# One subtraction of the first q, on its fourth slot, is moved from VectorE to POOL

## The chip, the cores and the metric

The kernel runs on one core of a Trainium2 chip, with a granted TensorE clock of 0.999. The metric is device time in microseconds (us), lower is better. Engines are called by the names that the profile uses: PE (TensorE matmul), PEld (its weight load), DVE (VectorE), ACT (ScalarE), POOL (GpSimd), SP (SyncE).

## What is computed

An attention of the "efficient" kind, whose output is the input of a two-layer feed-forward net with an ELU between the layers. Everything is float32 at the outside.

```python
# q, k, v: [8 batches, 8 heads, 576 rows, 64]
q_s = softmax(q, axis=-1)          # over the 64 columns of each row: max, subtract, exp, sum, divide
k_s = softmax(k, axis=2)           # over the 576 rows
kv  = einsum('bhsd,bhse->bhde', k_s, v)
attn = einsum('bhsd,bhde->bhse', q_s, kv)
x   = attn.transpose(0, 2, 1, 3).reshape(4608, 512)
h   = x @ w_in                     # w_in: 512 x 2048
g   = where(h > 0, h, exp(min(h, 0)) - 1)
out = g @ w_out                    # w_out: 2048 x 512
```

## The kernel before

Each batch gives 512 rows to the net in one pass of 16 hidden tiles (128 hidden units by 512 rows); the 64 rows left over of each batch are gathered into a ninth pass. For one hidden tile PE runs four matmuls with `W1S` (`hidden_mm`, L911), ACT the exponential into `ES` (L894, or L891 and L892 for the tiles of a list), POOL a small fix-up of `ES` (L895), DVE the combination of both into `GT` (`elu`, L924), and PE four matmuls with `W2S` that add to the output (`project`, L932). Projection runs three tiles behind. The softmaxes and small attention matmuls of the next batch are woven between these tiles by the tables `FIRST`, `SECOND` and `LATER`, written by hand: words such as `qsub:2:dve` name a step, a part and an engine.

The first batch has nothing to hide behind. Its steps are the words of one string, `START`, and `first_batch` issues them in that order. An engine executes its own instructions in the order of issue, and waits by semaphores for what it reads and overwrites (`op`, `need`). So the string fixes four or five queues at once: a word that moves in it moves in the queue of its own engine only, among the words of that engine.

In the first batch q and k lie in four slots of two heads each. For slot n of q the steps are `qmax:n` (DVE, L671), `qsub:n` (subtract the row's maximum in place in `QR`, L678), `qexp:n` (ACT, L683), `qsum:n` (sum and reciprocal, DVE, L688 and L690), `qmul` (times the reciprocal, into `QS`, as float16, L707: `qmul:A:dve` for slots 0 and 1 together on DVE, `qmul:2:gp` and `qmul:3:gp` on POOL). `pturn:A` and `pturn:B` turn `QS` on PE (L765), `pwide:A` and `pwide:B` copy that into `QT` on ACT (L787). On the side of k and v, `kexp` makes the exponentials (ACT, L537 and L532), `vconv:A` and `vconv:B` convert v into `VB` (ACT, L854, and POOL, L856), `kv:A` and `kv:B` multiply them (PE, L559), and `kfac:A` (DVE) and `kfac:B` (its reciprocal on DVE, L613, the scaling on ACT, L622) write `MB`. `att:f` multiplies `MB` with `QT` (PE, L804), `xc:f` copies the result into `XT` (L811 on DVE, L813 on ACT), and `h:2:4` and `h:0:2` start the first hidden tiles. `warm` is a matmul whose result is not used. `kmax2:AB` and the `qmax` behind it on DVE belong to the second batch.

The words `w1:a:b` and `w2:a:b` load chunks of the two weight matrices; they are DMAs issued by POOL (L255, L262), and each takes time in POOL's own queue. The loads of q, k and v are issued by SP (L277, L285, L293).

Before the change `qsub:0` and `qsub:2` run on POOL (word `gp`) and `qsub:1` and `qsub:3` on DVE. In DVE's queue `qsub:3` stands between `qsum:0` and `qmul:A`. In POOL's queue the order from there on is `qsub:2`, `w2:2:3`, `w1:6:9`, `vconv:B`, `qmul:2`, `qmul:3`, `w2:3:4`, `w2:4:6`. The later batches subtract k's maximum in `ksub`; all words for its part `R` that reach the lines below `b == 1` name `dve`.

Of the kernel before, what the change touches and what calls it, by code (L numbers as in the profile page):

```python
# [11 lines left out]
B, H, S, D = 8, 8, 576, 64  # L12
# [3 lines left out]
R = 4  # L16
# [29 lines left out]
         "w1:4:6 kacross:B kexp:S vconv:A:act kmin:A qsub:2:gp diag:act:B w2:2:3 qsum:0 kmin:B "  # L46
         "kexp:A load:V:0:3 kmin:T qexp:2 qsub:3:dve qmul:A:dve qsum:2 load:V:0:2 qexp:3 w1:6:9 "
         "qsum:3 vconv:B:gp load:K:1:M qmul:2:gp kexp:B kexp:T kv:A kfac:A:dve pturn:A kv:B "
         "pwide:A:act kfac:B:act warm:1:3 att:1 att:0 qmul:3:gp pturn:B xc:1:dve xc:0 h:2:4 "
         "pwide:B:act w2:3:4 att:2 att:3 xc:2 load:Q:1:A load:Q:1:R w2:4:6 h:0:2 xc:3 kmax2:AB ")  # L50
# [70 lines left out]
class Gen:  # L121
# [303 lines left out]
    def ksub(self, b, part, en="gp"):  # L425
        if b == 1:
            self.ksub_slot(part, en)
            return
        e, s = self.E[en], b % 2
        KR = self.KR[s]  # L430
        nm = self.NB[:, :].rearrange("p (h d) -> p h d", d=64)
        if part != "R":
            h0, n = {"A": (0, 4), "B": (4, 4)}.get(part) or (2 * int(part), 2)
            kv = KR[:, 4 * h0:4 * (h0 + n), :].rearrange("p (h r) d -> p h r d", r=R)
            m = nm[:, h0:h0 + n, :].unsqueeze(2).broadcast_to([128, n, R, 64])
            keys = self.kkeys(b, part)
            self.op(en, lambda: e.tensor_tensor(kv, kv, m, ALU.subtract), keys + ["NB"], keys)  # L437
        else:
            for i in range(2):
                sl = slice(64 * i, 64 * i + 64)  # L440
                kv = KR[sl, 32:36, :]
                m = nm[sl, 4 * i:4 * i + 4, :]
                self.op(en, lambda: e.tensor_tensor(kv, kv, m, ALU.subtract),
                        [f"KR{s}R{i}", "NB"], [f"KR{s}R{i}"])
# [762 lines left out]
```

## Time and profile before

| | us |
|---|---|
| three runs: median (lowest to highest) | 310.6 (310.38 to 311.41) |
| the profiled execution, device time | 310.93 |
| its span, first to last instruction | 308.9 |
| PE busy in the span | 297.4 (96%) |
| DVE busy | 237.0 (77%) |
| ACT busy | 193.2 (63%) |
| POOL busy | 170.4 (55%) |

The profiled execution has 2.03 us outside its span, and is 0.33 us above the median of the three runs. Line numbers are those of the kernel before; after the change, lines from 429 on are one higher. A row of the timeline gives the start in us, the duration in us, the engine, the line, the operation, its output and inputs with their shapes, how many instructions are merged in it, and in brackets how long the engine sat idle before and who released it. Rows of one engine overlap by up to 0.1 us, since the next instruction is taken up before the one in front of it has ended. The chain of waits is followed back from the last instruction; its rows are stretches that do not overlap.

### The profile page before, as it was taken

The page shows a single profiled execution, that of the slowest core. Times are in us where ns is not written, and L with a number is a line of the kernel's source. Part 1 is how long each engine was busy: PE and PEld are TensorE (multiplying, and loading weights), DVE is VectorE, ACT ScalarE, POOL GpSimd, SP SyncE. Part 2 cuts the span into 40 slices and gives each one's busy share as a digit, 9 for nine tenths or more (in the row PEclk, how much of TensorE's full clock was granted, in tenths as well). Part 3 has the DMA queues.
Part 4 walks back from the last instruction along what each step waited for, and adds up shares of the span by engine and source line. Part 5 has one row for each costly group of instructions (what it writes and reads, how often), then busy time and mean ns, then how long its engine had stood idle before and what let it go on. Part 6 is the DMA issues. An engine that isn't in the chain of part 4 may idle for free.

```text
span 308.9 us, 4839 instructions
## 1 busy us (share of the span) xinstructions
PE 297.4 (96%) x1733; PEld 239.8 (78%) x1733; DVE 237.0 (77%) x401; ACT 193.2 (63%) x358; POOL 170.4 (55%) x214
## 2 busy tenths in 40 slices
PE   6769999999999999999999999999999999999995
PEld 4457877688878888888888888888888888888884
DVE  6999998979959898899889998998895353335442
ACT  2578785577468885877587758775777543334432
POOL 2856785596535742786378636863696333333440
PEclk9999999999999999999999999999999999999999
DMA  7999999995707994668565856590503030003004
GB/s 229 397 346 334 373 360 272 255 250 166 205 3 227 271 233 129 210 133 209 157 208 147 207 148 198 146 187 23 172 17 62 2 136 0 0 2 136 0 0 136
DMA packets 60583, 51.63 MB, mean 167 GB/s; under 512 B 26896, under 2 KB 50704, under 8 KB 60560
## 3 DMA queue, kind: packets, MB, share of 16 engines
q1 hardware_dynamic: 52960, 41.23, 47.8%
q0 software_dynamic: 6400, 8.39, 10.3%
q10 hardware_dynamic: 1200, 1.72, 2.2%
q8 instruction: 13, 0.21, 0.3%
q14 instruction: 10, 0.08, 0.1%
HBM read 38.27 MB, written 9.45 MB: 154 GB/s over the span
## 4 chain that ended last, share of the span: by engine, by line
PE 90%; DVE 6%; DMA 2%; issue 1%; SPq 1%; ACT 0%
PE bank L932 43%; PE bank L911 42%; PE bank L826 2%; DMA QR<-in_q_dram 2%; DVE KT L326 2%; PE bank L597 1%; DVE QF L688 1%; DVE QS L707 1%; DVE QF L671 1%; PE bank L804 1%; SPq L277 1%; PE bank L559 0%; DVE QR L678 0%; DVE QM L671 0%; DVE KA L326 0%
## 5 line engine op out<-in xcount | busy, mean ns | idle before, releaser
L932 PE MATMUL bank<-W2S,GT 128*128 128x512 f32 x572 | 153.5, 392 | 0.2 <-DVE GT L924 0.2
L895 POOL TENSOR_SCALAR ES<-ES 128x512 f32<-128x512 f32 (+1 forms) x130 | 85.6, 661 | 116.2 <-ACT ES L894 116.1
L911 PE MATMUL bank<-XT,W1S 128*128 128x512 f32 x512 | 138.4, 393 | 0.8 <-issue 0.6
L924 DVE SCALAR_TENSOR_TENSOR GT<-bank,ES 128x512 fp32r<-128x512 f32 (+1 forms) x130 | 88.0, 681 | 53.1 <-PE bank L911 38.4
L932 PEld LDWEIGHTS bank<-W2S,GT 128*128 128x128 f32 x572 | 106.2, 188 | 22.3 <-DVE GT L924 0.6
L894 ACT ACTIVATE ES<-bank 128x512 f32<-128x512 f32 (+1 forms) x130 | 76.1, 593 | 70.3 <-PE bank L911 70.2
L911 PEld LDWEIGHTS bank<-XT,W1S 128*128 128x128 f32 x512 | 94.1, 188 | 20.2 <-ACT XT L813 0.9
L678 POOL TENSOR_TENSOR QR<-QR,QM 128x512 f32<-128x512 f32 (+1 forms) x21 | 24.9, 1188 | 0.6 <-DVE QM L671 0.6
L683 ACT ACTIVATE QR<-QR 128x1024 f32<-128x1024 f32 (+3 forms) x19 | 19.1, 1007 | 3.3 <-DVE QR L678 3.1
L854 ACT ACTIVATE XT<-bank 128x320 fp32r<-128x320 f32 (+1 forms) x30 | 15.0, 500 | 9.4 <-PE bank L826 9.4
L688 DVE TENSOR_REDUCE QZ<-QR 128x16 f32<-128x1024 f32 (+1 forms) x14 | 18.8, 1343 | 0.6 <-ACT QR L683 0.6
L671 DVE TENSOR_REDUCE QM<-QR 128x16 f32<-128x1024 f32 (+1 forms) x14 | 18.8, 1341 | 0.0
L911 PE MATMUL bank<-XTR,W1S 128*128 128x512 f32 x64 | 16.6, 389 | 0.0
L622 ACT ACTIVATE MB<-bank,KZ 64x64 fp32r<-64x64 f32 x44 | 10.1, 303 | 7.4 <-DVE KZ L613 7.3
L437 DVE TENSOR_TENSOR KR<-KR,NB 128x512 f32<-128x512 f32 x16 | 14.6, 938 | 0.0
L387 DVE TRANSPOSE_TENSOR_REDUCE KM<-KR 128x32 f32<-128x1024 f32 x12 | 14.4, 1225 | 0.0
L856 POOL CAST QT<-QW 128x1024 fp32r<-128x1024 f16 x12 | 12.5, 1038 | 2.7 <-DMA QW<-QS 2.7
L911 PEld LDWEIGHTS bank<-XTR,W1S 128*128 128x128 f32 x64 | 12.0, 188 | 2.5
L891 ACT ACTIVATE ES<-bank 128x512 f32<-128x512 f32 x15 | 8.9, 594 | 6.7 <-PE bank L911 6.7
L826 PE MATMUL bank<-QT,MB 128*128 128x320 f32 (+1 forms) x48 | 12.4, 300 | 0.7 <-ACT XT L854 0.7
L707 POOL TENSOR_TENSOR QS<-QR,QI 128x1024 f16<-128x1024 f32 (+1 forms) x7 | 12.5, 1786 | 0.4 <-DVE QI L690 0.4
L483 ACT ACTIVATE EK<-KR 128x1024 bf16<-128x1024 f32 x12 | 12.6, 1051 | 0.0
(108 smaller groups left out, 263.6 us busy)
## 6 DMA issues: line engine op xcount, KB each, us to landing
out_dram<-OSB SPq DMA_DIRECT2D x30, 256.0 KB, 2.7
KR<-in_k_dram SPq DMA_DIRECT2D x6, 1024.0 KB, 8.3
VR<-in_v_dram SPq DMA_DIRECT2D x6, 1024.0 KB, 6.2
QR<-in_q_dram SPq DMA_DIRECT2D x5, 1024.0 KB, 8.1
KR<-in_k_dram SPq DMA_DIRECT2D x8, 288.0 KB, 6.4
VR<-in_v_dram SPq DMA_DIRECT2D x8, 288.0 KB, 6.8
W1S<-in_moe_w_in_dram POOLq DMA_DIRECT2D x3, 768.0 KB, 9.5
QR<-in_q_dram SPq DMA_DIRECT2D x4, 512.0 KB, 9.7
```

The lines of the kernel that those rows point to most:

```text
L671: self.op("dve", lambda: v.tensor_reduce(m, QR, AX.X, ALU.max), self.qkeys(b, part), self.qstat("QM", b, part))
L678: self.op(en, lambda: e.tensor_tensor(QR, QR, m, ALU.subtract), keys + self.qstat("QM", b, part), self.qown(b, part))
L683: self.op("act", lambda: a.activation(QR, QR, AF.Exp), keys, self.qown(b, part))
L688: self.op("dve", lambda: v.tensor_reduce(z, QR, AX.X, ALU.add), self.qkeys(b, part), self.qstat("QZ", b, part))
L707: self.op(en, lambda: e.tensor_tensor(out, QR, z, ALU.mult), keys + self.qstat("QI", b, part), [f"QS{x}" for x in cells])
L826: last = pe.matmul(self.bank[bank][:, a - c0:b - c0], self.MB[f][:, :, :].rearrange("p u d -> p (u d)"), self.QT[:, f, a - f * S:b - f * S ...
L854: self.op("act", lambda: e.activation(out, src, AF.Copy), reads, writes)
L894: self.op("act", lambda: a.activation(ES[:, x], ps[:, x], AF.Exp), [f"bank{bank}"], keys + mark)
L895: self.op("gp", lambda: g.tensor_scalar(ES[:, x], ES[:, x], -1.0, 1.0, ALU.add, ALU.mult), keys, keys)
L911: return pe.matmul(ps, self.W1S[:, kc, c * 128:(c + 1) * 128], x[:, kc, 0:SM], start=(kc == 0), stop=(kc == 3))
L924: self.op("dve", lambda: v.scalar_tensor_tensor(out[:, x], *how), [f"bank{bank}"] + eks + (["FINE"] if n < FINE else []), keys)
L932: return pe.matmul(self.bank[OB[t]][:, :], self.GT[n % NG][:, t * 128:(t + 1) * 128], self.W2S[:, c, :], start=(c == 0), stop=(c == NCH - ...
```

## The change

The word `qsub:3:dve` is taken out of its place in front of `qmul:A:dve`, and `qsub:3:gp` is put directly behind `qsub:2:gp`, in front of the loads `w2:2:3` and `w1:6:9` in POOL's queue. A second edit sets the engine of `ksub` to DVE where the part is `R`; every such word names DVE already.

```diff
-         "w1:4:6 kacross:B kexp:S vconv:A:act kmin:A qsub:2:gp diag:act:B w2:2:3 qsum:0 kmin:B "
-         "kexp:A load:V:0:3 kmin:T qexp:2 qsub:3:dve qmul:A:dve qsum:2 load:V:0:2 qexp:3 w1:6:9 "
+         "w1:4:6 kacross:B kexp:S vconv:A:act kmin:A qsub:2:gp qsub:3:gp diag:act:B w2:2:3 qsum:0 kmin:B "
+         "kexp:A load:V:0:3 kmin:T qexp:2 qmul:A:dve qsum:2 load:V:0:2 qexp:3 w1:6:9 "
          "qsum:3 vconv:B:gp load:K:1:M qmul:2:gp kexp:B kexp:T kv:A kfac:A:dve pturn:A kv:B "
          "pwide:A:act kfac:B:act warm:1:3 att:1 att:0 qmul:3:gp pturn:B xc:1:dve xc:0 h:2:4 "
@@ ksub
         if b == 1:
             self.ksub_slot(part, en)
             return
+        en = "dve" if part == "R" else en
         e, s = self.E[en], b % 2
```

## The prediction

> **What bounds the kernel now.** I read the page's busy times first, then PE's waits from 26.7 us to the end, then the chain of waits over the first 40 us.
>
> ```profile
> PE 297.4 (96%) x1733; PEld 239.8 (78%) x1733; DVE 237.0 (77%) x401; ACT 193.2 (63%) x358; POOL 170.4 (55%) x214
> ...
> PE bank L826 <- ACT XT L854: 0.7, 1, 0.7
> PE bank L911 <- ACT XT L813: 0.2, 1, 0.2
> PE bank L932 <- DVE GT L924: 0.2, 1, 0.2
> ...
> 14.47 1.31 DVE QR L678
> 15.78 2.08 DVE QS L707
> ...
> 26.27 0.44 DVE GT L924
> 26.75 1.20 PE bank L932 x4
> ```
>
> The first row would say "PE, leave the rest alone". The three rows of waits sharpen it: after 26.7 us PE waits 1.1 us in all. So from the first projection at 26.75 us on, PE's work is packed, and whatever brings that moment forward or back moves the end with it, unless a later wait eats it. The last four rows say what sets that moment: before it the chain is on DVE, and the subtraction that the change moves (L678 at 14.47, `qsub:3`) is a link of it, directly in front of `qmul:A` (L707).
>
> **DVE: what is removed.** These are DVE's rows behind it.
>
> ```profile
> 14.39 1.39 DVE L678 TENSOR_TENSOR QR<-QR,QF 128x512 f32<-128x512 f32 x1
> 15.70 2.16 DVE L707 TENSOR_TENSOR QS<-QR,QF 128x1024 f16<-128x1024 f32 x1
> 17.78 0.67 DVE L688 TENSOR_REDUCE QF<-QR 128x8 f32<-128x512 f32 x1
> ...
> 18.61 0.64 DVE L688 TENSOR_REDUCE QF<-QR 128x8 f32<-128x512 f32 x1
> ...
> 19.55 0.61 DVE L628 SCALAR_TENSOR_TENSOR MB<-bank,KZ 64x128 fp32r<-64x128 f32 x2
> ```
>
> One instruction goes, and 1.31 us of the chain with it. But two durations here look long, so I looked for the same shapes elsewhere, and for what happens when DVE and POOL both work.
>
> ```profile
> 27.05 0.68 DVE L678 TENSOR_TENSOR QR<-QR,QM 128x512 f32<-128x512 f32 x1
> 75.95 1.21 DVE L707 TENSOR_TENSOR QS<-QR,QI 128x1024 f16<-128x1024 f32 x1
> ...
> 132.94 1.10 DVE L437 TENSOR_TENSOR KR<-KR,NB 128x512 f32<-128x512 f32 x1
> ...
> 132.18 1.31 POOL L437 TENSOR_TENSOR KR<-KR,NB 128x512 f32<-128x512 f32 x1
> 133.44 1.07 POOL L895 TENSOR_SCALAR ES<-ES 128x512 f32<-128x512 f32 x1
> ```
>
> Undisturbed, a DVE subtraction of this shape is 0.68 and a product of `qmul:A`'s size 1.21 us. The last three rows show the disturbance: the DVE subtraction from 132.94 ends at 134.04, 0.6 behind the end of POOL's own subtraction at 133.49. It stood still until POOL's instruction was over and then ran its usual length; and POOL's next instruction (1.07) stood behind DVE in turn. So a DVE operation with two inputs in SBUF and a POOL operation take turns, whole instructions at a time, and a waiting DVE instruction goes ahead of POOL's next one. By these rows `qsub:3` lost 0.71 us and `qmul:A` 0.95 us to POOL.
>
> **POOL: what is added.**
>
> ```profile
> 13.09 1.06 POOL L678 TENSOR_TENSOR QR<-QR,QF 128x512 f32<-128x512 f32 x1
> 14.09 0.58 POOL L262 DMA_DIRECT2D W2S<-in_moe_w_out_dram  x1
> 14.66 0.75 POOL L255 DMA_DIRECT2D W1S<-in_moe_w_in_dram  x1
> 15.40 1.38 POOL L856 CAST VB<-VR 128x1152 bf16<-128x1152 f32 x1
> 18.78 2.04 POOL L707 TENSOR_TENSOR QS<-QR,QF 128x512 f16<-128x512 f32 x2 [2.00 <-DVE QF L690]
> ```
>
> The same instruction on POOL is 1.06 us (`qsub:2`, the first row). Its input is ready: DVE was past the maxima when it took up the old `qsub:3` at 14.39. So it runs from 14.15 to 15.2, and everything behind it in POOL's queue moves by 1.06: the issue of `w2:2:3` and `w1:6:9`, then `vconv:B`, which starts at 16.46. `qmul:2` and `qmul:3` have cover, since POOL sat idle between 16.78 and 18.78.
>
> **The new order of the start.** `qmul:A` is taken up at 14.47, and now POOL's `qsub:3` is in its way until 15.2. Then it goes ahead of `vconv:B` by the rule of turns and needs 1.21: it ends at 16.4, where it ended at 17.86, so 1.46 earlier. From the end of `qmul:A` to the end of `kfac:A` (20.16 in the rows above) lie 2.30 us of DVE work, so `kfac:A` ends at 18.7. Whether its inputs come in time is read from ACT and PE.
>
> ```profile
> 15.23 1.21 ACT L683 ACTIVATE QR<-QR 128x512 f32<-128x512 f32 x2
> 17.30 0.28 ACT L532 ACTIVATE EK<-bank 128x128 bf16<-128x128 f32 x1
> 18.64 1.02 ACT L787 ACTIVATE QT<-bank 128x1024 fp32r<-128x1024 f16 x1 [1.07 <-PE bank L765]
> 20.39 1.04 ACT L622 ACTIVATE MB<-bank,KZ 64x64 fp32r<-64x64 f32 x4 [0.72 <-DVE KZ L613]
> 21.46 0.60 ACT L813 ACTIVATE XT<-bank 128x512 fp32r<-128x512 f32 x1
> ...
> 18.44 0.73 PE L559 MATMUL bank<-VB,EK 64*64 64x66 bf16 x36
> 19.10 0.50 PE L1092 MATMUL bank<-GT,ONES 128*128 128x512 f32 x1
> 20.21 0.74 PE L804 MATMUL bank<-QT,MB 128*128 128x512 f32 x2 [0.60 <-DVE MB L628]
> ```
>
> ACT's `qexp:2` and `qexp:3` end at 16.44 as before: `qexp:3` can start no earlier than behind `qexp:2`, so the earlier `qsub:3` (15.2 for 15.78) brings nothing there; `qsum:2` needs only `qexp:2`, done about 15.84, and `qsum:3` about 17.2 finds its input. ACT is busy until 17.58 (second row). `pwide:A` started 0.78 behind the end of `qmul:A`; that would be 17.2, so ACT's queue holds it until 17.58, and it ends at 18.6 instead of 19.66.
>
> `att:1` (PE, 20.21) needs `kfac:A` (18.7), `pwide:A` (18.6), and stands in PE's queue behind `kv:B` and `warm`. That is the link that becomes the last. `kv:B` needs `vconv:B`. Undisturbed I take `vconv:B` at 1.17, scaled from POOL's converting copy of a slightly smaller tile:
>
> ```profile
> 64.86 1.04 POOL L577 CAST VB<-VR 128x1024 bf16<-128x1024 f32 x1
> ```
>
> 1.04 x 1152 / 1024 = 1.17, and its own row, 1.38, which has a turn of DVE in it, is the other end. So it ends between 17.63 and 17.84, and `kv:B` starts about then instead of 18.44 (ACT's last exponential, 17.58, is in time). From the start of `kv:B` to the end of `warm` were 1.16 us (18.44 to 19.60): PE is free for `att:1` between 18.85 and 19.05. Hence `att:1` comes 1.15 to 1.35 earlier; 1.25 is the middle.
>
> The rest follows it. `xc:1` and the second batch's maxima on DVE stand back to back up to the first `elu` at 26.27. On ACT `kfac:B` starts behind its reciprocal, about 18.95, ends about 20.0, and `xc:0` ends about 20.6 instead of 22.06: earlier by more than 1.25, so no brake. `qmul:2` and `qmul:3` start at 17.84 and end at 19.9 instead of 20.82, and `pturn:B` and `pwide:B` fit behind `xc:0`. The first projection comes 1.25 earlier.
>
> **What could take it back later.** The weights come in one queue in order of issue. The tightest use that I found is the load of chunks 9 to 12 of `W2S`.
>
> ```profile
> W2S<-in_moe_w_out_dram POOLq DMA_DIRECT2D x1, 1024.0 KB, 14.4
> ...
> 30.31 0.75 POOL L262 DMA_DIRECT2D W2S<-in_moe_w_out_dram  x1
> ...
> 45.63 1.18 PE L932 MATMUL bank<-W2S,GT 128*128 128x512 f32 x4
> ```
>
> Issued at 30.31, it lands at 44.7, and PE wants it at 45.63: 0.9 us to spare. It is issued behind POOL's work on the first tiles, so its issue moves with them; if the landing moves too, nothing is lost, and if it stays, PE waits 1.25 - 0.9 = 0.35. I take 0.05. For the two loads that POOL now issues 1.06 later I see no cost: loads issued there take 10 us and more to land behind older ones (14.4 us for the big one). The second edit is nothing, since no instruction changes its engine.
>
> The sum: 1.25 - 0.05 = 1.2 us earlier. The profiled execution would be 310.93 - 1.2 = 309.73; it stands 0.33 above the median of the runs, so the median becomes 309.4. Bounds of the unknown terms alone: a gain of 0.8 (`vconv:B` at 1.38, the weights' 0.35) to 1.4, thus 309.2 to 309.8. About 0.3%, 0.93 us, is what a measurement of this kernel can tell from no change, so this is just over it.
>
> **The rivals.**
>
> First, an unseen hold in front of `qmul:A`. The row of `qsub:3` speaks for it: it stood 0.7 us from 14.47 to 15.16, when POOL's rows show only the issue of two DMAs (14.15 to 15.40). Something of POOL kept the way closed; perhaps parts of POOL were already at `vconv:B`. The Trainium skill, "GPSIMD Engine Reference", section "4. When to use GPSIMD", says that a pair of POOL's cores makes the descriptors of a DMA; the others could then have gone on, which no run here shows. If such a hold also follows the new `qsub:3`, `qmul:A` ends 0.7 later, at 17.1, `kfac:A` at 19.4, and `att:1` at 19.45 instead of 20.21: a gain of 0.76, median 309.85. Against it stand the rows from 132.18, where the waiting DVE went first. The Trainium skill, "SBUF — State Buffer", section "Who interferes with whom", says that the order of issue decides who is blocked, and for the whole instruction; by that rule `qmul:A` goes first and the sum stays, and those rows agree. Chance 0.2.
>
> Second, the other side: the turn is lost altogether. If `qmul:A` still stands at 16.46, when `vconv:B` is taken up, it stands until 17.84 and ends at 19.05, 1.19 later than before; `kfac:A`, `att:1` and all behind them follow: 310.6 + 1.2 = 311.8. The point from which it decides is plain: `qmul:A` must get its turn by 16.65 (17.86 - 1.21), or the change costs time. For it: `qmul:A` did wait out most of `vconv:B` before the change (2.16 for 1.21). Against it: that time `vconv:B` was first at 15.40. Chance 0.13.
>
> Third, the gain arrives at 26.75 and the weights take it back: the landing at 44.7 stays, and further loads behind it stay too. With one such wait of 0.35 and a second of as much, 0.5 us is left: 310.1. For it: the 0.9 us to spare is less than the gain. Against it: those loads are issued by the same tiles that come earlier. Chance 0.13.
>
> **How the numbers follow.** The forecast has what remains, 0.54; its time is 309.4. Faster by over 0.3% is most of the forecast (0.45, as a gain of 0.8 to 0.93 and the spread of the runs take some of it) and a part of the first rival (0.08): 0.53. Slower by over 0.3% is the second rival and a little for the spread: 0.15. Within 0.3%: 0.32. The range reaches from 308.9, a gain of 1.46 as on `qmul:A` itself with a little for the spread, to 311.0, which takes in the first and third rival and the case of no gain; the second rival lies outside.
>
> **What would show it.** Right, if in the profile after POOL has two rows of L678 behind each other from 13.1 to 15.2, `qmul:A` on DVE ends near 16.4 and lasts 1.9 with its wait, `vconv:B` ends by 17.9, the first `att` matmul is near 18.9 and the first projection near 25.5, and PE still waits about 1.1 us after it. Wrong at the first step, if `qmul:A` ends after 17; wrong at the end, if the projection is early but PE's waits have grown by as much; and wrong as a whole, if `att:1` waits for something that I have at no cost here, such as `vconv:B` beyond 18.4.

## The result, and the profile after

The changed kernel takes 309.95 us (median of 20 runs, 309.26 to 310.68); the kernel before, run beside it, 310.68 (20 runs, 309.91 to 312.91). The ratio is 0.9962, with a 95% interval of 0.9947 to 0.9977: faster by 0.7 to 1.6 us. The medians alone say 0.73. The forecast said 1.2 earlier and 309.4; the third rival, with the weights taking part of the gain back, said 310.1.

First the start in the profile after, the rows that answer to those of DVE, POOL and PE before (line numbers one higher from 429 on).

```profile
12.40 2.08 POOL L679 TENSOR_TENSOR QR<-QR,QF 128x512 f32<-128x512 f32 x2
13.82 1.75 DVE L708 TENSOR_TENSOR QS<-QR,QF 128x1024 f16<-128x1024 f32 x1
15.71 1.16 POOL L857 CAST VB<-VR 128x1152 bf16<-128x1152 f32 x1
16.82 2.06 POOL L708 TENSOR_TENSOR QS<-QR,QF 128x512 f16<-128x512 f32 x2
17.02 0.76 PE L560 MATMUL bank<-VB,EK 64*64 64x66 bf16 x36 [0.70 <-POOL VB L857]
17.27 0.61 DVE L629 SCALAR_TENSOR_TENSOR MB<-bank,KZ 64x128 fp32r<-64x128 f32 x2
18.05 0.62 PE L805 MATMUL bank<-QT,MB 128*128 128x512 f32 x2
24.47 1.20 PE L933 MATMUL bank<-W2S,GT 128*128 128x512 f32 x4 [0.15 <-DVE GT L925]
```

Both subtractions stand on POOL (x2), `qmul:A` is taken up at 13.82, stands until about 14.48, where POOL's second subtraction ends, and ends at 15.57, and PE's `kv:B` waits 0.70 for `vconv:B`. All of it stands earlier than forecast by one offset, though: in this execution loads of the first k and q landed earlier. DVE waited for them before, ahead of `qmax:0`, and does not after; this lies some 5 us ahead of the first word that moved. So starts are compared from `qmax:0`, the maximum of slot 0 (the first two rows are from before, the third from after):

```profile
6.68 0.43 DVE L326 TENSOR_TENSOR KT<-KR 128x256 f32<-128x256 f32 x1 [0.39 <-DMA KR<-in_k_dram]
8.14 0.69 DVE L671 TENSOR_REDUCE QF<-QR 128x8 f32<-128x512 f32 x1 [0.19 <-DMA QR<-in_q_dram]
7.45 0.69 DVE L672 TENSOR_REDUCE QF<-QR 128x8 f32<-128x512 f32 x1
```

| from `qmax:0` (us) | starts at | first projection at | between | from there to the end of the span |
|---|---|---|---|---|
| before | 8.14 | 26.75 | 18.61 | 282.15 |
| after | 7.45 | 24.47 | 17.02 | 283.63 |

The start became 1.59 us shorter, more than the 1.25 forecast; the rest became 1.48 longer. The length of the start does not hang on where `qmax:0` falls: in the profiles of e2, e5 and e9 below, where `qsub:3` stands as before the change, it is 18.62 to 18.64, and in those of e1, e6, e7 and e10, where it stands as after, 17.02 to 17.03, with `qmax:0` anywhere from 7.57 to 8.30. PE's waits after 20 us and the profile's chain show where the rest grew:

```profile
PE bank L933 <- DMA W2S<-in_moe_w_out_dram: 1.2, 2, 0.9
PE bank L827 <- ACT XT L855: 0.7, 1, 0.7
...
PE 85%; DMA 6%; POOL 4%; ACT 2%; DVE 2%; issue 1%
PE bank L933 40%; PE bank L912 40%; DMA W2S<-in_moe_w_out_dram 5%; PE bank L827 2%; POOL W1S L255 1%; PE bank L598 1%; DMA QR<-in_q_dram 1%; POOL QR L679 1%; POOL QS L708 1%; PE bank L805 1%; DVE KT L326 1%; DVE QF L672 0%; PE bank L560 0%; ACT ES L895 0%; ACT ES L893 0%
```

The first row is new: two waits for `W2S`, 1.2 us together (PE's rows overlap by up to 0.2, so a row of idle time is a little less than the time lost). DVE's 6% of the chain have become 2%, and a load of `W2S` stands in the chain instead. Which loads, and when they landed, is in the rows of PE and of the DMA issues; first those after, then those before.

```profile
37.57 1.19 PE L933 MATMUL bank<-W2S,GT 128*128 128x512 f32 x4 [0.95 <-DMA W2S<-in_moe_w_out_dram]
44.98 1.20 PE L933 MATMUL bank<-W2S,GT 128*128 128x512 f32 x4 [0.28 <-DMA W2S<-in_moe_w_out_dram]
25.71 0.76 POOL L262 DMA_DIRECT2D W2S<-in_moe_w_out_dram  x1
W2S<-in_moe_w_out_dram POOLq DMA_DIRECT2D x1, 768.0 KB, 11.8
28.02 0.76 POOL L262 DMA_DIRECT2D W2S<-in_moe_w_out_dram  x1
W2S<-in_moe_w_out_dram POOLq DMA_DIRECT2D x1, 1024.0 KB, 16.9
```

```profile
38.73 1.17 PE L932 MATMUL bank<-W2S,GT 128*128 128x512 f32 x4
28.00 0.76 POOL L262 DMA_DIRECT2D W2S<-in_moe_w_out_dram  x1
W2S<-in_moe_w_out_dram POOLq DMA_DIRECT2D x1, 768.0 KB, 9.5
```

The last column of a row of issues is the time from issue to landing. Chunks 6 to 8: issued at 28.00 before and 25.71 after, landed at 37.5 both times. Chunks 9 to 12: 44.7 before (30.31 + 14.4), 44.9 after. Issued 2.3 us earlier, they land at the same time. PE wants chunk 6 first; before, it came to it 1.2 us behind the landing; after, it stood idle for 0.95 us until the landing. At the first projection PE is 2.28 us ahead of the kernel before (24.47 for 26.75), at chunk 9 only 0.65 (44.98 for 45.63): all of the shorter start is gone there, and what is left is the early loads of k and q.

### The profile page after: what moved, and what is told of

Same layout as the page of the kernel before. It is cut to its first block, busy times and chain, and to the rows that moved or that the text cites. A ratio compares the mean times of both kernels' runs of the same rounds, so it can differ in the third digit from the quotient of the medians.

```text
span 308.1 us, 4839 instructions
## 1 busy us (share of the span) xinstructions
PE 297.6 (97%) x1733; PEld 240.1 (78%) x1733; DVE 235.0 (76%) x400; ACT 192.9 (63%) x358; POOL 171.3 (56%) x215
## 4 chain that ended last, share of the span: by engine, by line
PE 85%; DMA 6%; POOL 4%; ACT 2%; DVE 2%; issue 1%
PE bank L933 40%; PE bank L912 40%; DMA W2S<-in_moe_w_out_dram 5%; PE bank L827 2%; POOL W1S L255 1%; PE bank L598 1%; DMA QR<-in_q_dram 1%; POOL QR L679 1%; POOL QS L708 1%; PE bank L805 1%; DVE KT L326 1%; DVE QF L672 0%; PE bank L560 0%; ACT ES L895 0%; ACT ES L893 0%
## 5 line engine op out<-in xcount | busy, mean ns | idle before, releaser
L387 DVE TRANSPOSE_TENSOR_REDUCE KM<-KR 128x32 f32<-128x1024 f32 x12 | 14.4, 1226 | 0.0
```

## The experiments

The theory: the start is 1.6 us shorter because `qsub:3` and its turns with POOL left DVE, and PE's waits for weights keep a part of that. The rivals: the weights are not the bound and the gain is just smaller; or the rows of the start differ for another reason.

**The weights out of the way, in both kernels.** The same edit on the changed kernel (e1, and again e10) and on the kernel before (e2).

```diff
 FIRST
-    1: ("w1:13:14", "w1:9:12", "qsub:1:dve"),
+    1: ("", "w1:9:12", "qsub:1:dve"),
-    4: ("w1:12:13", "w2:9:13", "load:K:1:R qsum:A qsub0:R:dve"),
+    4: ("w1:12:14", "w2:9:11 w2:11:13", "load:K:1:R qsum:A qsub0:R:dve"),
```

Expected of e1: 

> The changed kernel, with two weight loads rearranged: chunk 13 of W1S, which nothing needs before tile 13, moves from the front of the queue to the load of chunk 12, and the load of chunks 9 to 12 of W2S is split in two. If the weights take the gain back (theory): PE's two waits for W2S (0.95 and 0.28 us after the change) go, and the time falls to about 1.5 us below the kernel before, some 0.7 below the changed kernel: about 309.2 where the kernel before has 310.7. If the weights are not what holds it (rival: the start simply gained only 0.7, the rest of the profile's difference being an early first load of q), the time stays at about 310.0 although the waits go.

Expected of e2: 

> The kernel before, with the same two weight loads rearranged, as the control of the first. In its profile PE waits nowhere for W2S, so the theory expects no change: within 0.3 us of 310.7. If the rearranged loads help by themselves (rival), it gains as much as the first does against the changed kernel, some 0.7 us.

Expected of e10: 

> The changed kernel with both weight loads rearranged, once more, as the version that is fastest so far: 308.94 in 7 executions. Theory: 308.7 to 309.2, no execution with a lower clock, ratio to the kernel before 0.991 to 0.995. Rival, that the first result owed to its chip: as the changed kernel, 309.9, ratio 0.996 to 0.998.

Measured: e1 308.94 us (7 runs), ratio to the kernel before 0.9931 (0.9905 to 0.9957); e10 308.92 (6 runs), 0.9916 (0.9893 to 0.9939); e2 312.11 (12 runs), 1.0016 (0.9992 to 1.0041). The number for e2 lies 1.4 above what was expected, because PE's mean clock was below 0.997 in 9 of its 12 executions (more on this below); the three at full clock took 310.66 to 310.94, as expected. The kernel before beside them has such executions too, which makes the ratios of e1 and e10 larger than the edit's own worth: its executions at full clock took 310.59 beside e1 (median), and e1 is 1.65 below that. The waits of e1:

```profile
PE bank L827 <- ACT XT L855: 0.7, 1, 0.7
PE bank L912 <- issue: 0.2, 1, 0.2
PE bank L912 <- ACT XT L814: 0.2, 1, 0.2
PE bank L933 <- DVE GT L925: 0.2, 1, 0.2
```

No wait for `W2S` is left. The start of e1 is 17.02 us (7.64 to 24.66), as after the change, and what follows takes 282.04, as before it. In e10, where `qmax:0` falls later than it did before (8.30), the start is 17.03 and the rest 281.97. So all of the shorter start arrives once the weights are out of the way, with or without an early first load, and the edit gives nothing to the kernel before, which came too late to need it. The theory stands. This is also the version that beats both kernels.

**One half of the edit at a time, on the changed kernel** (one execution each).

```diff
 e6:
-    1: ("w1:13:14", "w1:9:12",     4: ("w1:12:13", "w2:9:13",
+    1: ("", "w1:9:12",             4: ("w1:12:14", "w2:9:13",
 e7:
-    4: ("w1:12:13", "w2:9:13",
+    4: ("w1:12:13", "w2:9:11 w2:11:13",
```

Expected of e6: 

> The changed kernel, with chunk 13 of W1S alone moved back in the queue of loads. If the order in that queue makes PE's first wait (0.95 us for chunk 6 of W2S), that wait goes or falls below 0.3, and the second (0.28, chunk 9, which lands no earlier) grows to 0.9 or more. Rival: the landing is set by something else than this queue and the first wait stays.

Expected of e7: 

> The changed kernel, with the load of chunks 9 to 12 of W2S alone split in two. The first wait (0.95 us, chunk 6) stays, the second (0.28, chunk 9) goes; time within 0.3 us of the changed kernel less 0.28, about 309.7. Rival: the waits do not follow the loads one by one, and both stay or both go.

Measured: e6 309.77 us, e7 309.22 us. PE's longest waits, e6 first:

```profile
PE bank L933 <- DMA W2S<-in_moe_w_out_dram: 1.0, 1, 1.0
```

```profile
PE bank L933 <- DMA W2S<-in_moe_w_out_dram: 0.5, 1, 0.5
```

In e6 the wait left is at 44.88, for chunk 9: moving chunk 13 of `W1S` back cleared the first wait, and the time went to the second. In e7 it is at 37.37, for chunk 6, and the second has gone. Each half takes away the wait that it was meant for. The size of e7's first wait, 0.5 for the 0.95 expected, differs because its first projection was 0.25 later (24.72) and chunk 6 landed at 37.4; with that wait, its time lies 0.5 below the 309.7 expected, a miss that one execution cannot weigh. How far PE is ahead of the kernel before shows what each version keeps:

| us ahead of the kernel before | at the first projection | at chunk 9 |
|---|---|---|
| changed kernel | 2.28 | 0.65 |
| e6, chunk 13 of `W1S` moved back | 2.15 | 0.75 |
| e7, load split | 2.03 | 1.31 |
| e1, both | 2.09 | 2.06 |
| e10, both | 1.42 | 1.43 |

The queue is not as simple as the order in it, though: chunk 6 landed at 36.6 in e6, but at 35.2 and 35.7 in e1 and e10, where only the load behind it differs. Why that helps it is open.

**The moved subtraction left out** (e3): slot 3 keeps its maximum, on no engine is it subtracted.

```diff
-kmin:A qsub:2:gp qsub:3:gp diag:act:B
+kmin:A qsub:2:gp diag:act:B
```

Expected: 

> The changed kernel without the moved subtraction on either engine: slot 3 of the first q goes to the exponential with its maximum still in it. It prices POOL's hosting, and the hold in front of the product for slots 0 and 1. If POOL's whole-instruction turns are all that held DVE, that product lasts about 1.2 us instead of the 1.75 of the changed kernel, or 1.9 if the unseen hold of 0.7 us that stood in front of the old subtraction (two loads being issued, the conversion of v behind them) comes back. The start then comes 0.2 to 0.7 us earlier than in the changed kernel; with the weights as the bound (theory) the total does not follow: 309.7 to 310.1. If the start is the bound (rival), 309.3 to 309.6.

Measured: 309.79 us (10 runs), ratio 0.996 (0.9938 to 0.9982). DVE's and POOL's rows:

```profile
14.47 1.81 DVE L708 TENSOR_TENSOR QS<-QR,QF 128x1024 f16<-128x1024 f32 x1
14.05 0.59 POOL L262 DMA_DIRECT2D W2S<-in_moe_w_out_dram  x1
14.63 0.76 POOL L255 DMA_DIRECT2D W1S<-in_moe_w_in_dram  x1
15.37 1.91 POOL L857 CAST VB<-VR 128x1152 bf16<-128x1152 f32 x1
```

The start is 17.08 us (8.10 to 25.18), no shorter than with the subtraction on POOL. The reason is in the first row: without it the unseen hold is back, `qmul:A` lasts 1.81, and POOL's `vconv:B` 1.91 instead of 1.16. So POOL hosts the subtraction for nothing: it fills a time in which DVE would have stood anyway. The total stays at that of the changed kernel. As the start did not shorten by the 0.2 to 0.7 expected, the total says nothing on the weights; but PE's row at chunk 9 does.

```profile
44.87 1.19 PE L933 MATMUL bank<-W2S,GT 128*128 128x512 f32 x4 [0.42 <-DMA W2S<-in_moe_w_out_dram]
```

Here `qmax:0` is at 8.10, as it was before, so no early load is in the way: PE is 1.57 ahead at the first projection and 0.76 at chunk 9.

**What the hold is** (e4): `vconv:B` on ACT, in the kernel before.

```diff
-qsum:3 vconv:B:gp load:K:1:M
+qsum:3 vconv:B:act load:K:1:M
```

Expected: 

> The kernel before, with the conversion of the second half of the first v on ACT instead of POOL, for two rows of DVE: the subtraction for slot 3 (1.39 us before) and the product for slots 0 and 1 (2.16). If POOL's conversion of v was the cause of both, also of the unseen hold, they last 0.68 and 1.21. If the issue of the two loads on POOL made the hold of the subtraction, it stays at about 1.39 and only the product falls to 1.21. ACT gets 1.16 us more work in front of its last exponentials, so the time itself may go either way by 1 us.

Measured: 310.31 us in its one execution. The two rows of DVE, and POOL's:

```profile
14.03 0.64 DVE L678 TENSOR_TENSOR QR<-QR,QF 128x512 f32<-128x512 f32 x1
14.58 1.22 DVE L707 TENSOR_TENSOR QS<-QR,QF 128x1024 f16<-128x1024 f32 x1
13.72 0.58 POOL L262 DMA_DIRECT2D W2S<-in_moe_w_out_dram  x1
14.30 0.75 POOL L255 DMA_DIRECT2D W1S<-in_moe_w_in_dram  x1
```

The two loads are issued as before, beside DVE's subtraction, and it takes 0.64 instead of 1.39. So the issue of the loads is not the hold; `vconv:B`, standing ready behind them in POOL's queue, is, even while POOL's rows still show the loads. The Trainium skill, "GPSIMD Engine Reference", section "4. When to use GPSIMD", says that a pair of POOL's cores makes a DMA's descriptors. That the other cores go on to the next instruction meanwhile would fit these rows; no run here shows single cores.

e4 also says what the change won on DVE. With `qsub:3` still on DVE, `qmul:A` ends 8.02 us behind `qmax:0` (15.80 - 7.78), against 8.12 in the changed kernel and 9.72 before. So it was not the subtraction's own time: in the changed kernel DVE stands about as long for POOL's subtraction (13.82 to 14.48) as its own takes in e4 (0.64). What went are the two holds by `vconv:B`, 0.71 and 0.95 us. The start of e4 is 17.86 us, only 0.75 shorter, because ACT now carries `vconv:B` and PE waits 1.64 for ACT in front of `kv:B`.

**PE's clock in the start** (e5, e9, e8). The kernel before showed something the forecast did not deal with: in 23 of its 54 executions with a recorded clock the mean granted clock was 0.987 to 0.995, and those took 312.12 us (median) where the others took 310.68. They come in two sizes: 14 at 0.993 to 0.995 took 311.57, and 9 at 0.987 or 0.988 took 312.73. The changed kernel had no such execution in 20, nor had e1, e3, e6, e7 and e10 in 25. Two runs fill PE's gap of 1.44 us in the kernel before:

```diff
-kv:A kfac:A:dve pturn:A kv:B
+kv:A warm:3:3 kfac:A:dve pturn:A kv:B
```

Expected of e5: 

> The kernel before, with three more matmuls without use (1.2 us) on PE in the gap between the first product of k and v and the turn of q, where PE is idle for 1.44 us. In the runs so far the kernel before had a mean granted clock of 0.987 to 0.994 in 8 of 24 executions, which took about 312.1 us against 310.6 at 0.998 and more; the changed kernel had none in 20. If PE's idle time in the start decides on that (theory), executions with the lower clock become rare and those at full clock stay at 310.6. If the idle time has nothing to do with it (rival), about a third keep the lower clock.

Expected of e9: 

> The kernel before with the three extra matmuls in PE's gap once more, only to count. So far 1 of 10 executions had a mean clock below 0.997, against 13 of 37 of the kernel before without them. If PE's idle time in the start decides (theory), at most 1 or 2 of some 12 now, and again about a third of the kernel before on the same chip. If it is chance (rival), about 4 of 12.

Expected of e8, which is e2's kernel: 

> The kernel before with both weight loads rearranged once more, for one more profile: 9 of its 12 executions had a lower mean clock, and its profile so far was none of these. If this one is, the granted clock by stretch shows where it falls: in the start, if PE's idle time there decides (theory), and then for a stretch of some 3 to 8 us at half clock, by 0.6% to 1.3% of the span; spread over the span or at its end by the rival, that it is chance.

Measured: e5 310.78 us, ratio 0.9993 (0.9972 to 1.0014), 1 of 10 executions at the lower clock against 5 of 13 beside it; e9 310.6, ratio 0.9981 (0.9957 to 1.0006), 2 of 12 against 10 of 17. At full clock they take 310.57, as the kernel before. The one execution of e8 has the lower clock, 0.987, and took 312.8 us. Its busy time by stretch has PE's first and the granted clock third from the end:

```profile
16.00:20.00 4.00, 2.00 (x89) 1.52 (x81) 3.85 (x8) 2.43 (x5) 2.00 (x3) 0.95 1.30 323
20.00:24.00 4.00, 3.96 (x38) 2.91 (x39) 3.14 (x7) 2.64 (x6) 1.91 (x3) 0.50 1.38 372
24.00:27.00 3.00, 3.00 (x10) 2.35 (x9) 2.26 (x5) 1.08 (x2) 0.00 (x0) 0.59 1.44 378
```

PE ran at half clock for nearly 7 us, from about 19.6 to 26.5 (0.95 of the first stretch, 0.50 and 0.59 of the others), right behind the stretch in which it was busy for 2.00 of 4 us. The first projection came at 28.68, 20.73 behind `qmax:0` where 18.6 is usual, so this drop cost 2.1 us. The same stretch, shifted to the start of `qmax:0`, before, after and in e5:

```profile
16.00:20.00 4.00, 2.17 (x99) 1.70 (x93) 3.86 (x8) 2.60 (x5) 2.00 (x3) 1.00 1.29 326
```

```profile
15.32:19.32 4.00, 3.04 (x125) 2.45 (x121) 3.40 (x11) 3.58 (x10) 4.00 (x5) 1.00 1.28 326
```

```profile
15.63:19.63 4.00, 3.07 (x104) 2.19 (x96) 3.87 (x8) 2.62 (x5) 2.00 (x3) 1.00 1.29 329
```

PE is busy for 2.17 of 4 us before, 3.04 after, 3.07 with the matmuls without use. Less idle time, fewer drops: 3 of 22 against 15 of the 30 run beside them. The idle time makes the drop likelier and does not force it, since the profiles before and of e2 have the same 2.17 without a drop. The Trainium skill, "TensorE: Matmul & The Clock Gate", section "Part 1: The HAM clock gate", says that the clock halves after an idle window of about 3.4 us, whose position does not depend on the kernel; that the drop comes in some executions only agrees with that, though PE was not idle for a whole window here. Why the filled gap still let 3 through is open.

## Why the prediction was right, and where it was off

**What bounds the kernel, and the step on DVE**: right. The chain through `qsub:3` was the one to shorten, and e1 shows that all of its shortening reaches the end when no later wait eats it. But what left the chain was not the subtraction's time: it was the two holds by `vconv:B` (e4).

**The turns of DVE and POOL**: right in the outcome. `qmul:A` waited for `qsub:3` and went ahead of `vconv:B`. In the time since `qmax:0` it ended at 8.12 (15.57 - 7.45), where the forecast had 8.26 (16.4 - 8.14). The rule that a waiting DVE instruction goes ahead of POOL's next one was put to an easy test, though, since the issue of two loads stood between `qsub:3` and `vconv:B`. The first rival's hold did not come; e3 and e4 show that it is real, but follows the loads, and in the changed kernel `qmul:A` stood waiting (13.82) before they were issued (14.40). The second rival's point, a turn by 16.65, was reached with a wide margin: the turn came at 15.17 on the clock of the kernel before (14.48 + 0.69).

**The link that becomes the last**: right in kind, `kv:B` behind `vconv:B`. `kv:B` started 9.57 behind `qmax:0`, inside the 9.49 to 9.70 of the forecast. Mis-sized was the step from there to `att:1`, taken as 1.2 and measured as 1.03 (17.02 to 18.05; the forecast's own 1.16 would have put PE free at 18.79 to 19.00, not 18.85 to 19.05), and 0.1 more came behind it. The start gained 1.59 where 1.25 was forecast.

**What could take it back**: this is the step that failed. It named the mechanism, but looked at one load only, chunks 9 to 12, and took 0.05. The load in front of it, chunks 6 to 8, had 1.2 us to spare (38.73 against 37.5), and the assumption that a landing moves with its issue was wrong for both: they landed at 37.5 and 44.9. In the profiled execution the waits took all of the shorter start. Without its early loads the same working gives: with the start's 1.59, PE comes to chunk 6 at 37.14 and waits 0.4; with the 1.2 left it comes to chunk 9 at 44.4 and waits 0.3 to 0.5; 0.7 to 0.9 is kept. e3, which has no early load, kept 0.76 at chunk 9. The third rival had the kind and nearly the time, 310.1 for 309.95, at a chance of 0.13.

**The number**: two errors of the sum partly cancel, 0.35 too little for the start and some 0.7 too little for the weights; with the second alone the gain would have come out at about 0.5. And the range reached past no gain at all, so that the time lies inside it says little.

**A term that the sum has not**: the device time has a part outside the span, which the forecast took as unchanged. It is 2.0 to 2.1 us on average in the kernel before, e2, e5 and e9, and 1.8 after the change and in e1, e3 and e10. So of the 0.73 between the medians 0.2 to 0.3 lies outside the span, where no row shows its cause. Inside, the medians are 308.6 (the 31 executions of the kernel before at full clock) and 308.15: 0.45, somewhat less than the 0.7 to 0.9, and no row read here shows where the difference goes.

**The spread**: the forecast took the runs' spread as noise. Part of it is the half clock in the start, and its going is a gain that no step had. Against the executions of the kernel before that are known to be at full clock the changed kernel gains 310.68 - 309.95 = 0.73; that the ratio's 1.2 is more would fit drops among the 20 runs of the kernel before (two of them took 312.8 and 312.9), but their clocks are not recorded.

## What to carry to other kernels

When a start-up is shortened, the slack of every load that lands in the following stretch has to be read, not the tightest one that comes to mind, and a load that is issued earlier need not land earlier: here two loads issued 2.3 us earlier landed when they had before. A load that is needed late should not stand in front of one needed early, and a big load whose first chunk is wanted early can be split; that was worth 1.0 us here (309.95 to 308.94), but only after the start had been shortened. And an instruction can be free on an engine that looks slower for it: POOL's subtraction takes 1.06 us where DVE's takes 0.64, but it stands where POOL's conversion would have held DVE.

## What the runs showed of the hardware

- A POOL instruction that reads SBUF and stands ready behind DMA issues on POOL holds a DVE operation with two SBUF inputs while the issues are still in the rows: 1.39 us with `vconv:B` behind them, 0.64 without (e4). A DVE operation that stood waiting before the issues was not held: `qmul:A` of the changed kernel, 1.09 us from the end of POOL's subtraction to its own end.
- Issuing a load 2.3 us earlier, with others in front of it in POOL's queue of loads, did not move its landing: 37.5 us both times. That holds for this order of loads alone: with chunk 13 moved back and the next load split, in the kernel before, the same load issued at 27.20 (e2) and 29.20 (e8) landed at 36.2 and 38.1.
- The mean granted clock was below 0.997 in 23 of 54 executions of a kernel that kept PE busy for 2.17 of 4 us in one stretch of its start, and in none of 45 executions of kernels with the shorter start (3.04 us after the change). In the one such execution with a profile, PE ran at half clock for nearly 7 us, which cost 2.1 us; the 23 took 0.9 us more (14 of them) or 2.05 us more (9).
